# Scores of the narrow batches of a Nyström attention spread over all sixteen 32x32 tiles of the matmul engine

## The chip, the cores and the metric

The kernel runs on one core of one Trainium2 chip. The metric is device microseconds of one execution, compared by the median over runs. TensorE (PE) multiplies, with its weight loads listed apart (PEld); VectorE (DVE), ScalarE (ACT) and GpSimd (POOL) do the elementwise work; SyncE (SP) issues loads and stores, and GpSimd issues the loads of the expert weights.

## The reference, cut to what matters

Two stages follow one another. First comes Nyström attention over 8 batches, 8 heads, 576 tokens and head size 64, with 32 landmarks; a landmark is the mean of 18 consecutive tokens:

```
q_lm = q.reshape(B, H, m, S // m, D).mean(axis=3)      # m = 32, S // m = 18; k_lm likewise
A  = softmax(scale * q    @ k_lm^T)                    # 576 x 32
Bm = softmax(scale * q_lm @ k_lm^T)                    # 32 x 32
C  = softmax(scale * q_lm @ k^T)                       # 32 x 576
Z  = Bm^T / (norm1 * norminf); six times: Z = 2 Z - Z @ Bm @ Z
attn = A @ Z @ C @ v
```

Its output, one row of 512 for each of the 4608 tokens, goes into a mixture of 8 experts: a gate picks one expert for each token, and the token gets `gate * sigmoid * (relu(x @ w1[e]) @ w2[e])`. Inputs and outputs are float32.

## The kernel before, in words

**Batches and halves.** `attend(b, ...)` (line 631) handles one batch in two halves of four heads (`hf`). `solve` (line 830) iterates the inverse for a group of one or two batches; the groups are (0), (1), (2), (3), (4, 5), (6, 7). `finish` (line 936) routes a batch, has the weights of its most frequent expert brought, and computes that expert for the whole batch. Tokens that chose another expert are redone at the very end under a condition (lines 1193 on).

**Order of the work.** All operations are first registered with `P.op`, each with a cost for every engine that may do it, a priority and a load on the DMA queues. `Plan.run` (line 276) then lays out the whole program: it repeatedly takes the operation that can begin first on some engine, with ties broken by priority (`PR` for attention, `FR` for experts, and a table `OFF` with one offset for each operation), and picks the engine on which the operation would end first. The `shy` values add a penalty to one of the engines; `SHY = 1194.3494` ns is the penalty for putting a landmark sum on DVE instead of POOL. While PE would idle before 75 us, the planner puts in filler matmuls on a zero tile (line 572).

**Wide and narrow batches.** The first two batches (`PET = 2`) are wide: their q and k are transposed by PE, so that head size (64) lies on partitions together with the parity of the token, and scores contract over 64 rows at once. The other six are narrow, and the change is about them:

- *Loads* (`bring`, line 646, issued on SP). For q and k, partition = (head, landmark), and a partition holds the landmark's 18 tokens as one run of 18 x 64 floats (4608 bytes); one DMA for a half batch (line 652). For v, three DMAs with runs of six tokens (1536 bytes, line 649). Three buffers for each of q, k and v; at most four loads are in flight.
- *Transposes* (line 690, DVE). Blocks of 32x32 are turned, so that 32 of the head's 64 columns (half `j`) lie on a head's 32 partitions, with tokens along the free dimension.
- *Landmark sums* (`sums`, line 700): 18 tokens are added, on POOL by five additions (lines 704 to 708) or on DVE by one reduction (line 702). The result `s9` has 64 columns for each of q and k. Line 723 turns it into `lm`.
- *Scores* (`scores`, line 741): for each half of the tokens (`n`), half of the head size (`j`) and head (`h`) there are two matmuls of 32 rows, 32 columns and 288 moving columns, one for k into `pC` and one for q into `pA`:

```
def one(n, x, h, j, o, p, last):
    nc.tensor.matmul(p.t[o * m:(o + 1) * m, n, :U2], lhsT=l_of(...), rhs=t_of(...), start=(j == 0), stop=last)
...
one(n, "k", h, j, h, pC, j == 1)
one(n, "q", h, j, (h + 2) % HH, pA, j == 1)
```

Row block `h` of the array is used with column block `h` (k) and `(h + 2) % 4` (q): eight of the sixteen 32x32 tiles. A float32 matmul stands as two records in the trace, so a narrow score has 64 matmul records and 64 weight loads; a wide one has 32 of each, on eight tiles of 64x32.

After the scores, `C` goes through a maximum on DVE (line 760), an exponential on ACT (765), a transpose on PE (773) and the product with v (784, `pv`). `A` is turned by DVE (802), normalised by POOL and DVE (805 to 819), turned again (823) and kept as bf16 in `Ab` (602 or 604). The inverse is line 914 (`pinv`), the routing runs from 964 to 1037, the requests for weights are lines 579 and 582 (POOL), and the expert is in lines 1088 (`mix`), 1103 and 1114 (`up2`, `up`), 1131 and 1134 (`down`), 1143 or 1145 (scaling) and 1158 (output, SP).

Of the kernel before, what the change touches and what calls it, by code (L numbers as in the profile page):

```python
# [23 lines left out]
BF16 = mybir.dt.bfloat16  # L24
# [4 lines left out]
ADD = mybir.AluOpType.add  # L29
# [4 lines left out]
X = mybir.AxisListType.X  # L34
# [37 lines left out]
class Plan:  # L72
# [380 lines left out]
def kernel(  # L453
# [22 lines left out]
    HH = H // 2  # L476
    PT = 96
    NT = 5
    U2 = S // 2
    UP = NT * 128  # L480
    NH = S // 2
    SHY = 1194.3494
    SHYE = 106.9356
    SHYR = -121.5916
    SHYB = 336.6076
    PR = [-20.0647, -14.4829, -11.9595, -11.6984, -8.0902, -5.3768, 0.7543, 4.1562]
    FR = [8.161, 20.7685, 18.9146, 5.2084, 9.1678, 27.2014, 12.0329, 8.2172]
    PET = 2
# [785 lines left out]
```

## Time and profile before

| | |
|---|---|
| median of three runs | 249.31 us (245.78 to 250.73) |
| profiled execution | 249.05 us, span 247.4 us |
| granted PE clock, mean | 0.986 |
| DVE, ACT, POOL busy | 174.2, 150.2, 137.1 us |
| line 743 (scores), k and q: matmul records | 448 and 448 |
| DMA | 31057 packets, 48.96 MB, 198 GB/s on average |

The profile is one execution, recorded by the hardware. "Busy" counts the time in which an engine has an instruction in flight; for PE this is modelled from pipelined matmuls, so a busy PE can still be far from its peak. The chain is followed backwards from the last instruction: at each step to what released it, or to the instruction before it on its engine. In the rows of groups the columns are line, engine, operation, output <- input, shape, count, then busy microseconds, mean nanoseconds of one, and the idle time just before with what ended it. S and M are the two kinds of PSUM tiles.

### The profile page before, as it was taken

The page shows a single profiled execution, that of the slowest core. Times are in us where ns is not written, and L with a number is a line of the kernel's source. Part 1 is how long each engine was busy: PE and PEld are TensorE (multiplying, and loading weights), DVE is VectorE, ACT ScalarE, POOL GpSimd, SP SyncE. Part 2 cuts the span into 40 slices and gives each one's busy share as a digit, 9 for nine tenths or more (in the row PEclk, how much of TensorE's full clock was granted, in tenths as well). Part 3 has the DMA queues.
Part 4 walks back from the last instruction along what each step waited for, and adds up shares of the span by engine and source line. Part 5 has one row for each costly group of instructions (what it writes and reads, how often), then busy time and mean ns, then how long its engine had stood idle before and what let it go on. Part 6 is the DMA issues. An engine that isn't in the chain of part 4 may idle for free.

```text
span 247.4 us, 10058 instructions
## 1 busy us (share of the span) xinstructions
PE 227.4 (92%) x4155; PEld 140.5 (57%) x4156; DVE 174.2 (70%) x405; ACT 150.2 (61%) x371; POOL 137.1 (55%) x205
## 2 busy tenths in 40 slices
PE   8998989978997999999999998999999999999970
PEld 3667664645564455655576667766666565555530
DVE  3648879997998589997995789888672473334330
ACT  2667764458774568695696755854785495625330
POOL 2658966979598665867765598815450055020000
PEclk9999999999999799999999999999999999999996
DMA  6999999999999875984898466105990369999542
GB/s 247 273 324 267 297 245 223 216 292 301 269 221 248 230 226 151 235 279 123 227 317 212 133 151 174 29 3 87 192 238 27 86 101 207 231 252 236 150 128 70
DMA packets 31057, 48.96 MB, mean 198 GB/s; under 512 B 5408, under 2 KB 22816, under 8 KB 31008
## 3 DMA queue, kind: packets, MB, share of 16 engines
q1 hardware_dynamic: 19904, 37.34, 53.3%
q0 software_dynamic: 10720, 10.49, 26.7%
q8 instruction: 33, 0.54, 0.9%
q10 hardware_dynamic: 384, 0.46, 0.7%
q14 instruction: 16, 0.13, 0.2%
HBM read 61.90 MB, written 9.44 MB: 288 GB/s over the span
## 4 chain that ended last, share of the span: by engine, by line
PE 69%; DVE 12%; DMA 7%; ACT 5%; issue 3%; POOL 1%; POOLq 0%; DVEq 0%; ACTq 0%
PE M L1131 22%; PE S L743 9%; PE M L914 7%; PE M L1114 6%; PE S L1103 6%; DMA w<-in_moe_w_dram 5%; PE M L784 4%; DVE s L702 4%; PE S L773 3%; PE M L1134 3%; DMA nk<-in_k_dram 2%; PE M L964 2%; PE M L676 1%; PE S L1088 1%; DVE sm L816 1%
## 5 line engine op out<-in xcount | busy, mean ns | idle before, releaser
L1131 PE MATMUL M<-w,hT 128*128 128x512 bf16 x256 | 62.1, 383 | 0.2
L1131 PEld LDWEIGHTS <-hT 128*128 128x128 bf16 x256 | 23.7, 99 | 26.3 <-issue 3.3
L579 POOL DMA_DIRECT2D w<-in_moe_w_dram x26 | 13.0, 505 | 30.7 <-DVE M L1036 22.7
L1143 ACT ACTIVATE y<-M,co 128x512 f32<-128x512 f32 (+1 forms) x34 | 22.1, 655 | 12.9 <-PE M L1131 6.5
L743 PE MATMUL S<-Tk,lm 32*32 32x288 f32 (+1 forms) x448 | 29.3, 405 | 0.0
L743 PE MATMUL S<-Tq,lm 32*32 32x288 f32 (+1 forms) x448 | 28.8, 404 | 0.0
L914 PE MATMUL M<-X 32*32 32x96 f32 (+1 forms) x768 | 23.4, 243 | 2.6 <-ACT X L928 1.8
L810 POOL TENSOR_TENSOR At<-At,sm 128x576 f32<-128x576 f32 x16 | 18.6, 1164 | 10.6 <-DVE sm L789 8.2
L914 PEld LDWEIGHTS M<-X 32*32 32x32 f32 x768 | 16.2, 105 | 11.9 <-ACT X L928 6.6
L600 ACT ACTIVATE hT<-M 128x288 bf16<-128x288 f32 x44 | 17.4, 421 | 9.1 <-PE M L1114 8.8
L1114 PE MATMUL M<-Ab_all,U 128*128 128x288 bf16 x128 | 22.8, 287 | 0.0
L819 POOL TENSOR_TENSOR At<-At,sm 128x576 f32<-128x576 f32 x16 | 18.6, 1161 | 6.1 <-DVE sm L817 4.0
L1103 PE MATMUL S<-Ab_all,U 128*128 128x288 bf16 x128 | 20.9, 286 | 0.6 <-ACT U L602 0.5
L928 ACT ACTIVATE X<-M 128x192 f32<-128x192 f32 (+1 forms) x34 | 13.2, 387 | 13.2 <-PE M L914 12.7
L602 ACT CAST U<-S 128x1024 bf16<-128x1024 f32 x16 | 16.0, 1015 | 4.1 <-PE S L1088 4.1
L704 POOL TENSOR_TENSOR s<-nq 128x576 f32<-128x576 f32 x13 | 18.4, 1412 | 0.0
L743 PEld LDWEIGHTS S<-Tk,lm 32*32 32x32 f32 (+1 forms) x448 | 14.7, 105 | 6.4 <-issue 1.1
L705 POOL TENSOR_TENSOR s<-s 128x256 f32<-128x256 f32 x23 | 16.8, 729 | 1.8
L704 POOL TENSOR_TENSOR s<-nk 128x576 f32<-128x576 f32 x10 | 14.2, 1418 | 5.6 <-DMA nk<-in_k_dram 5.6
L760 DVE TENSOR_REDUCE sm<-S 128x1 f32<-128x576 f32 x16 | 11.9, 743 | 7.1 <-PE S L743 7.0
L572 PE MATMUL M<-idle 128*128 128x512 bf16 x59 | 15.8, 415 | 1.1 <-DVE idle L585 1.1
L606 DVE TENSOR_SCALAR hT<-M 128x288 bf16<-128x288 f32 x20 | 8.8, 449 | 11.4 <-PE M L1114 11.2
(133 smaller groups left out, 486.5 us busy)
## 6 DMA issues: line engine op xcount, KB each, us to landing
nk<-in_k_dram SPq DMA_DIRECT2D x16, 576.0 KB, 6.9
nq<-in_q_dram SPq DMA_DIRECT2D x16, 576.0 KB, 6.8
nv<-in_v_dram SPq DMA_DIRECT2D x48, 192.0 KB, 5.8
w<-in_moe_w_dram POOLq DMA_DIRECT2D x16, 512.0 KB, 16.9
out_dram<-y SPq DMA_DIRECT2D x122, 64.0 KB, 4.0
w<-in_moe_w_dram POOLq DMA_DIRECT2D x20, 256.0 KB, 9.9
w<-in_moe_w_dram POOLq DMA_DIRECT2D x3, 1024.0 KB
out_dram<-y SPq DMA_DIRECT2D x30, 32.0 KB, 4.4
```

The costliest lines, as they stand in the source:

```text
L600: nc.scalar.activation(out=dst(), in_=src(), func=RELU)
L602: nc.scalar.copy(dst(), src())
L704: nc.gpsimd.tensor_tensor(s3.t, n.t[:, :9], n.t[:, 9:], op=ADD)
L705: nc.gpsimd.tensor_tensor(s3.t[:, :4], s3.t[:, :4], s3.t[:, 4:8], op=ADD)
L743: nc.tensor.matmul(p.t[o * m:(o + 1) * m, n, :U2], lhsT=l_of(lm, wide, 0 if x == "k" else 1, h, n if wide else j), rhs=t_of(Ts[x], x, wide ...
L810: P.op({"POOL": 1115}, lambda e, At=At, st=st: nc.gpsimd.tensor_tensor(At.t, At.t, b_l(st.t[:, 8:8 + g]), op=SUB), r=[st["ax"]], w=[At[0]] ...
L819: P.op({"POOL": 1115}, lambda e, At=At, st=st: nc.gpsimd.tensor_tensor(At.t, At.t, b_l(st.t[:, 32:32 + g]), op=MUL), r=[st["as"]], w=[At[0 ...
L914: nc.tensor.matmul(pN.t[r_, u * W + lo:(u + 1) * W], lhsT=cur.t[r_, u, :m] if it else nx.t[r_, u], rhs=cur.t[r_, u, lo:], start=(it == 0 a ...
L1103: nc.tensor.matmul(ph.t[:, n, :NH], lhsT=Uw.t[:, hf, fc * 128:(fc + 1) * 128], rhs=Ab.t[:, hf, n * NH:(n + 1) * NH], start=(hf == 0), stop ...
L1114: nc.tensor.matmul(ph.t[:, :NH], lhsT=Uw.t[:, hf, fc * 128:(fc + 1) * 128], rhs=Ab.t[:, hf, n * NH:(n + 1) * NH], start=(hf == 0), stop=(h ...
L1131: nc.tensor.matmul(py.t, lhsT=hTs[fc].t[:, i * 128:(i + 1) * 128], rhs=w2.t[:, fc, :], **f)
L1143: nc.scalar.activation(out=y.t[:, :n], in_=py.t[:, :n], func=COPY, scale=com.t[:, i:i + 1])
```

## The change

Only narrow batches change their data layout. Partitions of q and k become (token half `a`, head parity `l`, landmark `r`), and a partition holds two heads with nine tokens each (runs of 2304 bytes), in two DMAs. Sixteen tiles are then addressed by the scores: row block 2n+l, column block 2hh+l for k, and its neighbour for q. A landmark's sum now lies in two halves on partitions 64 apart, so that new copies (ACT or POOL) bring each half to the other's partitions and an addition on POOL completes it; the landmark transpose covers 256 columns instead of 128. v is loaded with runs of three tokens in six DMAs. The head order of `pA`, and with it lines 953, 1086 and 1223, becomes `h ^ 1`. Output rows of the narrow batches follow the new token order. The planner's costs for the changed operations, its priorities, penalties and offsets are replaced as well. The two `Ag` tiles of the conditional end are taken from `hT`. The diff, without the offsets and the conditional end:

```diff
-    SHY = 1194.3494
-    SHYE = 106.9356
-    SHYR = -121.5916
-    SHYB = 336.6076
-    PR = [-20.0647, -14.4829, -11.9595, -11.6984, -8.0902, -5.3768, 0.7543, 4.1562]
-    FR = [8.161, 20.7685, 18.9146, 5.2084, 9.1678, 27.2014, 12.0329, 8.2172]
+    SHY = 167.6745
+    SHYE = 109.3114
+    SHYR = -145.2341
+    SHYB = 2451.9822
+    PR = [-26.8602, -20.7218, -20.3964, -10.8075, -9.8749, 3.0349, 6.2307, 13.5424]
+    FR = [4.6994, 24.0288, 15.8812, 17.8203, 24.5648, 28.2369, 14.8052, 5.6756]
...
-    FILL = 1.2174
+    FILL = 1.2515
-    AFF = 0.1761
+    AFF = 0.3677
...
+                        elif x == "v":
+                            i_ = [nc.sync.dma_start(out=n.t[w * m:(w + 1) * m, :, a * 3 * D:(a + 1) * 3 * D],
+                                                    in_=s_.rearrange("h (r a w t) d -> a w r h (t d)", a=2, w=3, t=3)[a, w])
+                                  for a in range(2) for w in range(3)]
+                        elif not wide:
+                            i_ = [nc.sync.dma_start(out=n.t[a * D:(a + 1) * D].rearrange("p (h t) d -> p h (t d)", h=2),
+                                                    in_=s_.rearrange("(h l) (r a t) d -> a (l r) h (t d)", l=2, a=2, t=g // 2)[a])
+                                  for a in range(2)]
...
+                        if not wide:
+                            f, o = n.t.rearrange("p (h t) d -> p h t d", h=2), s9.t[:, i].rearrange("p (h d) -> p h d", h=2)
+                            if e == "DVE":
+                                nc.vector.tensor_reduce(o, f.rearrange("p h t d -> p h d t"), axis=X, op=ADD)
+                                return
+                            a = s3.t[:, :8].rearrange("p (h t) d -> p h t d", h=2)
+                            nc.gpsimd.tensor_tensor(a, f[:, :, :4], f[:, :, 4:8], op=ADD)
+                            nc.gpsimd.tensor_tensor(a[:, :, :2], a[:, :, :2], a[:, :, 2:4], op=ADD)
+                            nc.gpsimd.tensor_tensor(a[:, :, 0], a[:, :, 0], a[:, :, 1], op=ADD)
+                            nc.gpsimd.tensor_tensor(o, a[:, :, 0], f[:, :, 8], op=ADD)
+                            return
...
+                    def cross(e, s9=s9, other=other):
+                        for a in range(2):
+                            o, i_ = other.t[a * D:(a + 1) * D], s9.t[(1 - a) * D:(2 - a) * D]
+                            if e == "ACT":
+                                nc.scalar.copy(o, i_)
+                            else:
+                                nc.gpsimd.tensor_copy(o, i_)
+                    P.op({"ACT": 570, "POOL": 800}, cross, r=[s9[0], s9[1]], w=[other[0]], prio=pr + .02)
+                    P.op({"POOL": 600}, lambda e, s9=s9, other=other: nc.gpsimd.tensor_tensor(s9.t, s9.t, other.t, op=ADD),
+                         r=[other[0]], w=[s9[0], s9[1]], prio=pr + .02)
+                    P.op({"DVE": 330}, lambda e, lm=lm, s9=s9: nc.vector.transpose(
+                        out=lm.t.rearrange("p x r -> p (x r)"), in_=s9.t.rearrange("p x d -> p (x d)")),
...
+                    for j in range(2):
                         for n in range(2):
+                            for l_ in range(2):
+                                r_ = slice((2 * n + l_) * m, (2 * n + l_ + 1) * m)
+                                for hh in range(2):
+                                    c = 2 * hh + j
+                                    for i, (x, p) in enumerate((("k", pC), ("q", pA))):
+                                        o = 2 * hh + l_ if x == "k" else (2 * hh + l_) ^ 1
+                                        f = Ts[x].t[r_, j, hh * U2:(hh + 1) * U2]
+                                        nc.tensor.matmul(p.t[o * m:(o + 1) * m, n, :U2], lhsT=lm.t[r_, i, c * m:(c + 1) * m],
+                                                         rhs=f.rearrange("p (w c r) -> p c w r", w=3, r=m) if x == "k" else f,
+                                                         start=(j == 0), stop=(j == 1))
-                P.op({"PE": 980 if wide else 1950}, scores, recs=64 if wide else 128,
+                P.op({"PE": 980 if wide else 1010}, scores, recs=64 if wide else 128,
```

More of the change, by code (lines that the diff above doesn't have):

```diff
@@ L636, in attend @@
             lms, ATs = lms_of[b], ATs_of[b] = [], []
+            wide = b < PET
             for hf in range(2):
@@ L657, in bring @@
                                               reason="loads in flight")
-                    loads[me] = P.op({"SP": 470 if x != "v" else 1350}, bring, w=[n[0]], prio=pr if x != "v" else pr + .15, lag=2000,
+                    loads[me] = P.op({"SP": (1350 if wide else 2650) if x == "v" else 470 if wide else 850}, bring, w=[n[0]], prio=pr if x != "v" else pr + .15, lag=2000,
                                       load=(2500.0 if x == "v" else LOAD), after=behind)
@@ L666, in attend @@
                 Ts = {"q": Val(t_T["q"]), "k": Val(t_T["k"])}
-                wide = b < PET
                 if wide:
@@ L689, in attend @@
                     for x in "kq":
-                        P.op({"DVE": 1265}, lambda e, T=Ts[x], n=ns[x], x=x: nc.vector.transpose(
-                            out=T.t.rearrange("p j (t r) -> p t j r", r=m) if x == "q" else
-                            T.t.rearrange("p j (t w r) -> p w t j r", t=6, w=3),
-                            in_=n.t.rearrange("p t (j c) -> p t j c", j=2) if x == "q" else
-                            n.t.rearrange("p (w t) (j c) -> p w t j c", j=2, w=3)),
+                        P.op({"DVE": 1265}, lambda e, T=Ts[x], n=ns[x]: nc.vector.transpose(
+                            out=T.t.rearrange("p j (t r) -> p t j r", r=m), in_=n.t.rearrange("p t (j c) -> p t j c", j=2)),
                             r=[ns[x][0]], w=[Ts[x][u] for u in range(3)], prio=pr + .01)
@@ L722, in attend @@
                 else:
-                    P.op({"DVE": 205}, lambda e, lm=lm, s9=s9: nc.vector.transpose(
-                        out=lm.t[:, 0], in_=s9.t.rearrange("p x d -> p (x d)")),
+                    other = Val(t_sw)
+                    def cross(e, s9=s9, other=other):
[10 more added lines that the diff above has]
+                        out=lm.t.rearrange("p x r -> p (x r)"), in_=s9.t.rearrange("p x d -> p (x d)")),
                         r=[s9[0], s9[1]], w=[lm[0]], prio=pr + .02)
@@ L730, in attend, with t_of @@
                 st = Val(t_sm)
-                def t_of(T, x, wide, n, h, j):
-                    if wide:
-                        f = T.t.rearrange("p a c -> p (a c)").rearrange("p (t c) -> p t c", c=128)[n * D:(n + 1) * D, :, h * m:(h + 1) * m]
-                        return f.rearrange("p (w c) r -> p c w r", w=3) if x == "k" else f
-                    f = T.t[h * m:(h + 1) * m, j]
-                    if x == "k":
-                        return f.rearrange("p (c n u) -> p n c u", n=2, u=PT)[:, n]
-                    return f.rearrange("p (t n r) -> p n t r", n=2, r=m)[:, n]
+                def t_of(T, x, n, h):
+                    f = T.t.rearrange("p a c -> p (a c)").rearrange("p (t c) -> p t c", c=128)[n * D:(n + 1) * D, :, h * m:(h + 1) * m]
+                    return f.rearrange("p (w c) r -> p c w r", w=3) if x == "k" else f
                 def scores(e, pC=pC, pA=pA, lm=lm, Ts=Ts, wide=wide):
-                    def one(n, x, h, j, o, p, last):
-                        nc.tensor.matmul(p.t[o * m:(o + 1) * m, n, :U2], lhsT=l_of(lm, wide, 0 if x == "k" else 1, h, n if wide else j),
-                                         rhs=t_of(Ts[x], x, wide, n, h, j), start=(j == 0), stop=last)
                     if wide:
@@ L748, in scores @@
                                 for n in range(2):
[L749 to L756 removed]
+                                    o = h if x == "k" else h ^ 1
+                                    nc.tensor.matmul(p.t[o * m:(o + 1) * m, n, :U2], lhsT=l_of(lm, True, "kq".index(x), h, n),
+                                                     rhs=t_of(Ts[x], x, n, h))
+                        return
+                    for j in range(2):
+                        for n in range(2):
+                            for l_ in range(2):
[9 more added lines that the diff above has]
+                P.op({"PE": 980 if wide else 1010}, scores, recs=64 if wide else 128,
                      r=[lm[0]] + [Ts[x][u] for x in "kq" for u in range(3)], w=[pC[0], pA[0]], hold=[EC, At, st],
@@ L779, in attend, with v_of @@
                 pV = Val(p_M, "attn", CAPA)
+                def v_of(c, wide=wide):
+                    return c if wide else c % 2 * 3 + c // 2
                 def pv(e, pV=pV, ECT=ECT, n=ns["v"]):
@@ L1186 @@
     U, Mb = t_U.tiles[0], pool.tile([128, 128], BF16, name="Mg")
-    Ab = [pool.tile([128, S], BF16, name=f"Ag{i}") for i in range(2)]
+    Ab = t_hT.tiles[FCH:FCH + 2]
     rows = pool.tile([128, B, NT], F32, name="rows")
```

37 lines of the change are left out of this document (17 added, 20 removed), and 263 rows, old and new, of the table OFF.

## The prediction

> **What bounds the kernel now.** I read the busy shares and the chain first, then busy time by stretches, then single groups. The page, PE being the matmul engine:
>
> ```profile
> PE 227.4 (92%) x4155; PEld 140.5 (57%) x4156; DVE 174.2 (70%) x405; ACT 150.2 (61%) x371; POOL 137.1 (55%) x205
> PE 69%; DVE 12%; DMA 7%; ACT 5%; issue 3%; POOL 1%; POOLq 0%; DVEq 0%; ACTq 0%
> ```
>
> The chain that ended last is PE for 69%. A busy PE includes filler matmuls (line 572), so the stages have to be told apart. Busy time in three stretches, then line 572 alone in the first two:
>
> ```profile
> 0.00:60.00 60.00, 52.81 (x976) 33.91 (x978) 44.53 (x89) 34.77 (x95) 43.34 (x70) 1.00 1.04 268
> 60.00:180.00 120.00, 115.47 (x2540) 72.77 (x2541) 102.43 (x238) 82.13 (x215) 82.17 (x120) 0.99 0.75 186
> 200.00:248.00 48.00, 39.43 (x293) 22.04 (x290) 16.94 (x46) 20.42 (x37) 7.98 (x12) 0.96 0.86 175
> ...
> 0.00:60.00 60.00, 15.83 (x59) 6.07 (x59) 1.00 1.04 268
> 60.00:200.00 140.00, 0.00 (x0) 0.00 (x0) 0.99 0.71 175
> ```
>
> Columns: length, busy PE, weight loads, DVE, ACT, POOL, then clock, DMA share, GB/s. Up to 60 us PE is not the limit: 15.83 us of its 52.81 is filler. From 60 to 180 us there is no filler and PE is busy 115.47 of 120; DVE has 102.43 (85%), ACT and POOL 68%. So between 60 us and the end a microsecond less of PE work can be a microsecond less of time, if the other engines follow. The pieces of the chain that matter:
>
> ```profile
> 29.81 1.21 PE S L743 x32
> 43.33 13.31 DMA w<-in_moe_w_dram
> 111.19 2.10 PE S L743 x64
> 118.78 2.10 PE S L743 x64
> 194.73 1.22 PE M L964 x32
> 231.53 6.91 PE M L1131 x32
> 238.44 1.01 PE M L1134 x16
> ```
>
> A narrow score (one half batch, batches 2 to 7) takes 2.10 us of the chain with 64 records; a wide one (batches 0 and 1), 1.21 us with 32. The last routing is at 194.73 us, and a pure expert stage follows it.
>
> **The scores: the gain.** Line 743 by stretches: the wide ones alone, then eleven of the twelve narrow ones:
>
> ```profile
> 0.00:40.00 40.00, 4.82 (x128) 1.99 (x128) 1.00 0.98 273
> 60.00:180.00 120.00, 24.54 (x704) 14.12 (x704) 0.99 0.75 186
> ```
>
> 4.82 / 4 = 1.21 us for a wide score, 24.54 / 11 = 2.23 us for a narrow one, neighbours' overlap included. Inside one narrow score:
>
> ```profile
> 48.40 0.42 PE L743 MATMUL S<-Tk,lm 32*32 32x288 f32 x4
> 48.51 0.44 PE L743 MATMUL S<-Tq,lm 32*32 32x288 f32 x4
> 48.64 0.42 PE L743 MATMUL S<-Tk,lm 32*32 32x288 f32 x4
> 48.75 0.44 PE L743 MATMUL S<-Tq,lm 32*32 32x288 f32 x4
> 48.88 0.42 PE L743 MATMUL S<-Tk,lm 32*32 32x288 f32 x4
> ```
>
> Eight records, one for each tile in use, repeat every 0.24 us: eight rounds for 64 records. The code before uses eight 32x32 tiles (rows h; columns h and h+2). After, row block is 2n+l and column block 2hh+l for k and its neighbour for q: sixteen different tiles, as many matmuls of the same size, hence four rounds. Four rounds less are 4 x 0.24 = 0.96 us a score, which leaves 1.14 us. The wide score is the nearest row: four rounds too, 1.21 us, with four tiles beside each other in each half of the rows, so four moving streams for a row block are already read at once there. Issue is no obstacle: a round now would need sixteen records in 0.24 us. Eleven scores lie after 60 us: 11 x 0.96 = 10.6 us. Ends: 11 x (2.10 - 1.21) = 9.8 and 11 x (2.23 - 1.21) = 11.2 us; I take 10.6. The twelfth lies at 48 us, where filler would take its place: nothing.
>
> The Trainium skill, page "TensorE: Matmul & The Clock Gate", section "Measured speedup vs the span model", gives 10.6 times for sixteen 32x32 tiles. An estimate from that page: 64 x 0.24 / 10.6 = 1.45 us for a score, and a gain of 11 x 0.65 = 7.2 instead of 10.6, a time of 244.0 instead of 240.6. The wide score's 32 records in 1.21 us with eight tiles lie at 6.3 times, nearly eight but for the start, so I follow the row.
>
> **The landmark sums and the crossing: added work off PE.**
>
> ```profile
> L705 POOL TENSOR_TENSOR s<-s 128x256 f32<-128x256 f32 x23 | 16.8, 729 | 1.8
> L704 POOL TENSOR_TENSOR s<-nk 128x576 f32<-128x576 f32 x10 | 14.2, 1418 | 5.6 <-DMA nk<-in_k_dram 5.6
> L706 POOL TENSOR_TENSOR s<-s 128x128 f32<-128x128 f32 x23 | 10.5, 456 | 1.8
> L708 POOL TENSOR_TENSOR s<-s 128x64 f32<-128x64 f32 x23 | 7.4, 321 | 1.8
> L702 DVE TENSOR_REDUCE s<-nk 128x64 f32<-128x1152 f32 x6 | 13.0, 2167 | 2.9 <-DMA nk<-in_k_dram 2.9
> L723 DVE STREAM_TRANSPOSE lm<-s 128x128 f32<-128x128 f32 x12 | 3.1, 275 | 0.0
> L802 DVE STREAM_TRANSPOSE At<-S 128x576 f32<-128x576 f32 x16 | 12.3, 767 | 0.6 <-PE S L743 0.6
> L602 ACT COPY lm<-M 128x256 f32<-128x256 f32 x3 | 1.1, 367 | 0.6 <-PE M L718 0.6
> ```
>
> A sum on POOL was 1418 + 729 + 456 + 2 x 321 = 3.25 us. Now it is 512 columns (between the rows of 256 and 576: 1.28 us) + 729 + 2 x 456 = 2.92 us, 0.33 less. On DVE it reads the same 1152 columns: 2.17 us, unchanged. Added for each score: two copies of 64x256 (bounded by ACT's 128x256: 2 x 0.37 = 0.73 us on ACT; on POOL at most 2 x 0.73) and one POOL addition of 128x256, 0.73 us. The landmark transpose grows from 128 to 256 columns: between 275 and 767 ns, 416, so 0.14 more on DVE. For twelve scores: DVE +1.7, ACT +8.8, POOL +8.8 less up to 24 x 0.33 = 7.9. From 60 to 180 us DVE then asks 104 of the 109.4 us that are left, 95%; ACT has 27 us of room in the shorter stretch and POOL as much, and the order may put evictions (lines 600 and 606) and sums on either side. I cost the work at nothing, covered by that room, but not the added latency. Sum to score grows by about 0.73 + 0.73 + 0.14 - 0.33 = 1.3 us. After 60 us another batch's expert matmuls fill PE while it passes; before 60 us nothing does. One narrow score feeds work there: 1.3 us at most, and I take 1.0. If all twelve showed it would be 15.6 us; less than nothing is excluded, since each path has one step more.
>
> **Transposes, tiles' order, planner.** Both big transposes now have q's form. They cost the same:
>
> ```profile
> L690 DVE STREAM_TRANSPOSE Tk<-nk 128x1152 f32<-128x1152 f32 x12 | 16.2, 1349 | 0.0
> L690 DVE STREAM_TRANSPOSE Tq<-nq 128x1152 f32<-128x1152 f32 x12 | 16.0, 1336 | 0.0
> ```
>
> The h^1 instead of h+2 in lines 953, 1086 and 1223 keeps count and size: nothing. All priorities, offsets and shyness values change; they move work without adding any.
>
> **Loads.**
>
> ```profile
> nk<-in_k_dram SPq DMA_DIRECT2D x16, 576.0 KB, 6.9
> nv<-in_v_dram SPq DMA_DIRECT2D x48, 192.0 KB, 5.8
> ...
> 46.85 1.28 SPq L649 DMA_DIRECT2D nv<-in_v_dram  x3
> 48.30 0.35 SPq L652 DMA_DIRECT2D nq<-in_q_dram  x1
> ...
> SPq L1158 <- ACT y L1143: 37.6, 13, 10.2
> ```
>
> The 24 narrow q and k loads become two DMAs each, and twelve v loads six instead of three: 24 x 0.35 + 12 x 1.28 = 23.8 us more on SP's queue. SP stood waiting 37.6 us for the outputs of line 1143, so its time is there; queued behind are outputs, whose buffers are six: nothing to 1 us, I take nothing. The runs halve, 4608 to 2304 bytes for q and k and 1536 to 768 for v. The v loads with 1536-byte runs land 576 KB no later than k with 4608-byte runs (5.8 us after issue, three issues 0.85 us apart, against 6.9), so q and k should lose nothing. 768 bytes has no row. At best nothing; at worst twice v's time per byte, in which case the first weight load (13.31 us on the chain, at DMA share above 1) could come 3 us later. I take nothing, by the nearest row.
>
> **Instruction fetch.** The chain has 3% "issue", and the page one queue of PE's size:
>
> ```profile
> q8 instruction: 33, 0.54, 0.9%
> ```
>
> 33 fetches for 8311 PE instructions, about 256 each. The twelve scores hold 1536 of them, now consumed twice as fast. If the waits (2.5% to 3%, some 6.5 us) grow with the speed of that 18%, it is 1.1 us more. Ends: nothing, and six fetches that each cost a whole saving, 5.8 us. I take 1.1, as most fetches fall elsewhere.
>
> **The sum.** The profiled execution took 249.05 us, span 247.4 and 1.65 around it; the median of the three runs is 249.31, 0.26 more. 249.05 - 10.6 + 1.0 + 1.1 = 240.55, say 240.6 us.
>
> **Rivals.**
>
> A. PE's freed time turns into waits. DVE at 95% of the shortened stretch cannot finish attention earlier, and expert work is not there to fill in. For it: DVE's 85% now. Against it: expert work for batches 4 and 5 still runs after 194.73 us, so there is stock to draw on. Four fifths lost: 249.05 - 2.1 = 247 us.
>
> B. Sixteen tiles do not run at once. Row blocks 2n and 2n+1 write the same PSUM bank in different partitions; if such writes excluded each other, each round would split in two and scores stay at 2.1 us. With the costs above: 249.05 + 1.0 = 250 us. Against it: the records at 48.40 us, where four row blocks already write one bank and eight records still repeat in 0.24 us; for it, that no row shows sixteen. The Trainium skill, page "TensorEngine Tiling (Array Packing)", section "Gotcha 1: PSUM Pressure", says that different row tiles cannot use one PSUM bank simultaneously; by that rule this rival would hold, and this trace disagrees with it for eight tiles.
>
> C. Slower: DVE becomes the bound. The value that keeps sums off DVE falls from 1194 to 168. If all 24 narrow sums went there, about fifteen more than the nine that it has now (six of k in the row above, and three of q), DVE takes on 15 x 2.17 + 1.7 = 34.3 us, some 31 of it after 60 us. Its room to 180 us is 120 - 102.4 = 17.6, so it decides from about seven moved sums. With all fifteen, attention ends 31 - 17.6 = 13.4 us later, near 209. After it stand two batches of experts, about 13 us until the weights land (the 13.31 above) and 8 us of end. A batch of experts is 37% of the chain over eight batches (lines 1131, 1114, 1103 and 1134 below): 0.37 x 247.4 / 8 = 11.4 us. So 209 + 22.9 + 13.3 + 8 + 1.65 = 255 us. Against it: the planner gives a sum to whichever engine ends first, and POOL, at 68%, would take sums back.
>
> ```profile
> PE M L1131 22%; PE S L743 9%; PE M L914 7%; PE M L1114 6%; PE S L1103 6%; DMA w<-in_moe_w_dram 5%; PE M L784 4%; DVE s L702 4%; PE S L773 3%; PE M L1134 3%; DMA nk<-in_k_dram 2%; PE M L964 2%; PE M L676 1%; PE S L1088 1%; DVE sm L816 1%
> ```
>
> **How the numbers follow.** Forecast 0.62, with its own range of 236 to 244: from 249.05 - 11.2 with no cost, less 2 us for a better order, to 249.05 - 9.8 + 5. Better still, under 236: 0.04. A 0.14, B 0.08, C 0.12. Faster by over 2% (below 244.3; 2% is about what a measurement tells from no change): 0.62 + 0.04 = 0.66; within 2%: A and B, 0.22; slower: C, 0.12. The range reaches from 235 to 251, over the forecast, A and B, and leaves out C.
>
> **What would show it.** Right: line 743's successor has 64 records in 1.1 to 1.3 us on the chain; after 60 us PE is still busy for 95% with no filler; the last routing comes a few us before 194.73 or at it, with less expert work behind it. Wrong: scores near 2 us (B); PE idle, or filler past 60 us, with DVE over 95% (A); more than seven extra sums in DVE's row for 128x1152 and a last routing past 200 us (C); first weights landing after 58 us (loads). The fetch term shows as "issue" between records of one score.

## The result, and the profile after

| | before | after |
|---|---|---|
| median of 4 runs, us | 248.25 (245.78 to 250.73) | 262.13 (261.04 to 263.46) |
| profiled execution, us | 249.05, span 247.4 | 261.04, span 259.4 |
| last routing on the chain, us | 194.73 | 206.35 |

The ratio is 1.0597, 95% interval 1.0483 to 1.0711: the changed kernel is slower, by 14 us, where a gain of 8 was forecast. Times are medians of all executions; a ratio leaves out executions that ran in a slower state, so it need not be the quotient of two medians, and where the two differ the text goes by the ratio.

The page of the changed kernel: busy time of each engine, then the chain that ended last by engine and by line:

```profile
PE 223.3 (86%) x4132; PEld 137.6 (53%) x4154; DVE 189.3 (73%) x412; ACT 155.2 (60%) x388; POOL 127.1 (49%) x181
...
PE 56%; DMA 26%; ACT 6%; issue 4%; DVE 2%; POOL 1%; SPq 1%; POOLq 0%; DVEq 0%; ACTq 0%
PE M L1174 20%; DMA nq<-in_q_dram 12%; DMA nk<-in_k_dram 8%; DMA nv<-in_v_dram 6%; PE M L1157 6%; PE M L957 5%; PE S L1146 5%; PE S L793 5%; PE M L1177 3%; PE M L827 3%; PE S L813 2%; ACT sw L756 1%; PE M L1007 1%; PE M L695 1%; PE S L1131 1%
```

PE did get 4.1 us less to do (223.3 instead of 227.4), and DMA went from 7% to 26% of the chain, with the loads of q, k and v as its three lines. Where the idle time lies shows in the stretch from 60 to 200 us, first of the kernel before:

```profile
60.00:200.00 140.00, 135.16 (x2891) 84.53 (x2889) 112.78 (x273) 94.97 (x241) 85.78 (x124) 0.99 0.71 175
```

and in the same view of the changed kernel (length, PE, weight loads, DVE, ACT, POOL, clock, DMA share, GB/s):

```profile
60.00:180.00 120.00, 104.01 (x2337) 65.89 (x2347) 103.67 (x228) 86.49 (x223) 81.94 (x112) 0.96 0.83 187
60.00:200.00 140.00, 123.60 (x2797) 78.56 (x2809) 118.07 (x255) 97.88 (x252) 86.79 (x118) 0.97 0.80 180
```

PE's idle time from 60 to 200 us grows from 4.8 to 16.4 us, by 11.6; the last routing comes 11.6 us later, and behind it 53 us follow as before. So the whole loss lies ahead of the last routing, and it is idle time of PE, not work. DVE is not full: 103.67 of 120. What PE waited for stands in the chain by time (start, length):

```profile
31.36 8.37 DMA nq<-in_q_dram
...
39.75 4.59 DMA nk<-in_k_dram
...
46.28 6.99 DMA nk<-in_k_dram
...
53.28 9.58 DMA nv<-in_v_dram
...
63.65 9.28 DMA nk<-in_k_dram
...
72.94 5.74 DMA nv<-in_v_dram
...
78.70 12.82 DMA nq<-in_q_dram
...
91.66 1.28 POOL s L723
...
136.30 3.31 issue
...
206.35 1.22 PE M L1007 x32
```

From 31 to 92 us the chain is one load after another. It ends at a landmark sum on POOL (line 723), for which POOL waits 10.4 us in three waits on loads of q, and after it come the steps that the change added. The timeline there (start, length, instruction, idle before it and its releaser):

```profile
91.66 1.27 POOL L723 TENSOR_TENSOR s<-nq 128x512 f32<-128x512 f32 x1 [4.05 <-DMA nq<-in_q_dram]
...
94.84 0.83 ACT L756 COPY sw<-s 64x256 f32<-64x256 f32 x2 [2.69 <-POOL s L726]
97.31 0.73 POOL L760 TENSOR_TENSOR s<-s,sw 128x256 f32<-128x256 f32 x1
...
101.57 0.42 DVE L762 STREAM_TRANSPOSE lm<-s 128x256 f32<-128x256 f32 x1
```

The copies, the addition and the transpose take 2 us together, yet 6.7 us lie between the start of the copies and the transpose. Over the eleven scores whose copies run on ACT it is 3.4 to 10.9 us, 7.5 in the mean. POOL and DVE hardly wait there (0.1 us of idle time ahead of all additions, 0.0 ahead of all transposes, in the rows below): other work lies between. The planner laid the steps apart so that the crossing would be covered, and that means that the sum, and the load ahead of it, is wanted that much earlier. The groups of the added work:

```profile
L756 ACT COPY sw<-s 64x256 f32<-64x256 f32 x22 | 8.9, 405 | 6.5 <-POOL s L726 5.5 <-DVE s L720 0.6
L760 POOL TENSOR_TENSOR s<-s,sw 128x256 f32<-128x256 f32 x12 | 8.8, 734 | 0.1
L762 DVE STREAM_TRANSPOSE lm<-s 128x256 f32<-128x256 f32 x12 | 5.0, 419 | 0.0
L723 POOL TENSOR_TENSOR s<-nk 128x512 f32<-128x512 f32 x9 | 11.5, 1276 | 0.7 <-DMA nk<-in_k_dram 0.4 <-DMA nq<-in_q_dram 0.2
```

These are near the sizes of the prediction: 0.41 us a copy (0.37 forecast), 0.73 the addition, 0.42 the transpose, 1.28 the first step of the sum. The scores themselves, line 793 from 60 to 200 us:

```profile
60.00:200.00 140.00, 20.14 (x704) 10.28 (x704) 0.97 0.80 180
```

11 scores at 1.83 us, where they took 2.23. That is 4.4 us of PE saved, not 10.6.

### The profile page after: what moved, and what is told of

Its sections match the earlier page's. It is cut to its first block, busy times and chain, and to the rows that moved or that the text cites. A ratio compares the mean times of both kernels' runs of the same rounds, so it can differ in the third digit from the quotient of the medians.

```text
span 259.4 us, 10165 instructions
## 1 busy us (share of the span) xinstructions
PE 223.3 (86%) x4132; PEld 137.6 (53%) x4154; DVE 189.3 (73%) x412; ACT 155.2 (60%) x388; POOL 127.1 (49%) x181
## 4 chain that ended last, share of the span: by engine, by line
PE 56%; DMA 26%; ACT 6%; issue 4%; DVE 2%; POOL 1%; SPq 1%; POOLq 0%; DVEq 0%; ACTq 0%
PE M L1174 20%; DMA nq<-in_q_dram 12%; DMA nk<-in_k_dram 8%; DMA nv<-in_v_dram 6%; PE M L1157 6%; PE M L957 5%; PE S L1146 5%; PE S L793 5%; PE M L1177 3%; PE M L827 3%; PE S L813 2%; ACT sw L756 1%; PE M L1007 1%; PE M L695 1%; PE S L1131 1%
## 5 line engine op out<-in xcount | busy, mean ns | idle before, releaser
L1174 PE MATMUL M<-w,hT 128*128 128x512 bf16 x235 | 60.4, 385 | 1.9 <-issue 1.0
L862 POOL TENSOR_TENSOR At<-At,sm 128x576 f32<-128x576 f32 x16 | 18.6, 1160 | 16.4 <-DVE sm L860 13.1
L957 PEld LDWEIGHTS M<-X 32*32 32x32 f32 x768 | 15.8, 104 | 16.4 <-ACT X L971 9.8
L971 ACT ACTIVATE X<-M 128x192 f32<-128x192 f32 (+1 forms) x35 | 13.6, 387 | 16.9 <-PE M L957 16.4
L793 PE MATMUL S<-Tk,lm 32*32 32x288 f32 x384 | 21.6, 431 | 0.0
L793 PE MATMUL S<-Tq,lm 32*32 32x288 f32 x384 | 21.1, 432 | 0.0
L610 ACT ACTIVATE hT<-M 128x288 bf16<-128x288 f32 x38 | 14.9, 418 | 5.4 <-PE M L1157 5.3
L616 DVE TENSOR_SCALAR hT<-M 128x288 bf16<-128x288 f32 x26 | 11.2, 452 | 9.1 <-PE M L1157 8.0
L813 PE MATMUL S<-I,EC 128*96 128x128 f32 x96 | 14.3, 286 | 2.8 <-ACT EC L805 2.6
L827 PE MATMUL M<-nv,ECT 96*32 96x64 f32 x768 | 15.0, 227 | 1.9 <-issue 1.5
L709 DVE STREAM_TRANSPOSE Tk<-nk 128x1152 f32<-128x1152 f32 x12 | 16.3, 1356 | 0.0
L709 DVE STREAM_TRANSPOSE Tq<-nq 128x1152 f32<-128x1152 f32 x12 | 16.0, 1342 | 0.0
L827 PEld LDWEIGHTS M<-nv,ECT 96*32 96x32 f32 x768 | 12.2, 113 | 6.9 <-ACT ECT L612 3.5
```

What stands on the lines that cost most here:

```text
L709: P.op({"DVE": 1265}, lambda e, T=Ts[x], n=ns[x]: nc.vector.transpose(out=T.t.rearrange("p j (t r) -> p t j r", r=m), in_=n.t.rearrange("p ...
L793: nc.tensor.matmul(p.t[o * m:(o + 1) * m, n, :U2], lhsT=lm.t[r_, i, c * m:(c + 1) * m], rhs=f.rearrange("p (w c r) -> p c w r", w=3, r=m) ...
L813: nc.tensor.transpose(pE.t[:PT, c // 3, (c % 3) * 128:(c % 3 + 1) * 128], in_=EC.t[:, c % 2, c // 2 * PT:(c // 2 + 1) * PT], identity=I128)
L827: nc.tensor.matmul(pV.t[h * m:(h + 1) * m, :D], lhsT=ECT.t[:, c, h * m:(h + 1) * m], rhs=n.t[:, h, v_of(c) * D:(v_of(c) + 1) * D], start=( ...
L862: P.op({"POOL": 1115}, lambda e, At=At, st=st: nc.gpsimd.tensor_tensor(At.t, At.t, b_l(st.t[:, 32:32 + g]), op=MUL), r=[st["as"]], w=[At[0 ...
L957: nc.tensor.matmul(pN.t[r_, u * W + lo:(u + 1) * W], lhsT=cur.t[r_, u, :m] if it else nx.t[r_, u], rhs=cur.t[r_, u, lo:], start=(it == 0 a ...
```

## The experiments

Two theories stood at the start. The first: the new loads are slower, and attention waits for them. The second: the added steps between sum and score (the crossing) hold attention up. Beside them stood the new order as a whole, and the size of the gain.

**What sixteen tiles are worth.** A kernel with only the score matmuls, on zeros, everything else left out. Each form ran five times, a row of independent matmuls ahead of each.

```
for j in range(2):                     # sixteen tiles
    for n in range(2):
        for l in range(2):
            for hh in range(2):
                for x in range(2): ... row block 2n+l, column block 2hh+l or its neighbour
```

> Only score matmuls on zero data (the rest of the computation is left out), each variant five times between filler matmuls. If the sixteen-tile score is limited by issue (a pair of weight load and matmul every 18 to 19 ns), the variants with sixteen tiles all take 1.2 us from first to last start, in any order of tiles, the strided k the same, and those with 144 and 32 columns take about as long. If it is limited by streaming or by shared PSUM banks, 144 columns take near half, and the variant in which each row block writes a bank of its own comes near 0.84 us (three rounds of 0.24 and the issue of the last). Eight tiles: 1.77 us as in the kernel before. The burst of six scores shows instruction fetch: over 1.6 us a score if fetch limits it.

Busy time of five scores of each form: eight tiles (line 87), sixteen (96), sixteen with a bank for each row block (122), sixteen with 144 columns (131) and with 32 (140):

```profile
0.00:265.00 265.00, 10.85 (x320) 5.44 (x320) 1.00 0.01 3
...
0.00:265.00 265.00, 8.01 (x320) 4.04 (x320) 1.00 0.01 3
...
0.00:265.00 265.00, 8.01 (x320) 4.04 (x320) 1.00 0.01 3
...
0.00:265.00 265.00, 5.61 (x320) 3.61 (x320) 1.00 0.01 3
...
0.00:265.00 265.00, 3.77 (x320) 3.15 (x320) 1.00 0.01 3
```

A score goes from 2.17 to 1.60 us: 0.57 saved, not 0.96. The order of the tiles and k's strided columns changed nothing, nor did a bank for each row block. From the first start to the last, 63 steps, it is 1.77 us with eight tiles and 1.20, 0.84 and 0.56 us with sixteen at 288, 144 and 32 columns. So a record costs 28 ns with eight tiles and 19, 13 and 9 ns with sixteen, and four rounds of 0.24 us is not what sixteen tiles reach. Six scores back to back took 1.58, 1.72, 2.11, 1.74, 2.76 and 1.89 us, each from its first start to its last end: between the matmuls there are holes, the longest of 1.17 us. Whether these are instruction fetches is not shown; no fetch record of this trace lies in the longest one.

**What PE time is worth.** In the kernel before, half of each narrow score's contraction is left out (32 records on eight tiles).

```diff
-for j in range(2):
+for j in range(1):
```

> The kernel before with the second half of each narrow score's contraction left out, so that 32 records instead of 64 run on the same eight tiles in the same order of work. A score then takes about 1.2 us instead of 2.17. If PE's time after 60 us is the time of the kernel, as the prediction said: 249 - 10.6 = 238 us. If freed PE time turns into waits for other engines: 245 to 248 us.

240.51 us, ratio 0.9689 (0.9592 to 0.9786). Line 743 in this kernel, 60 to 180 us:

```profile
60.00:180.00 120.00, 13.40 (x336) 5.78 (x321) 1.00 0.81 198
```

10.5 scores at 1.28 us, 0.95 less than the 2.23 before; for eleven scores 10.5 us of PE. By the ratio the time fell by 7.7: a microsecond of PE is worth 0.7. What took over shows in the chain of this kernel, where DVE, 12% before, has 24%:

```profile
PE 48%; DVE 24%; DMA 9%; ACT 8%; POOL 5%; issue 3%; SPq 0%; POOLq 0%; DVEq 0%; ACTq 0%
```

**The loads, one property at a time**, in the kernel before and in its order. First, the 24 narrow q and k loads in two DMAs of 64 partitions each, runs as long as before:

```diff
+i_ = [nc.sync.dma_start(out=n.t[a * D:(a + 1) * D],
+          in_=s_[2 * a:2 * a + 2].rearrange("h (r t) d -> (h r) t d", t=g)) for a in range(2)]
```

> The kernel before with each narrow q and k load cut into two DMAs of 64 partitions with the same runs of 4608 bytes; order of work unchanged. If loads into 64 partitions are the slow ones (about 240 instead of 390 GB/s, as the landings of the changed kernel suggest), a load takes 2.4 instead of 1.5 us and the time rises by 4 to 8 us. If the length of the runs does it, or the loads do not matter: within 1 us of before.

252.38 us, ratio 1.0165 (1.0057 to 1.0273). Second, two DMAs of all 128 partitions, with runs half as long:

```diff
+i_ = [nc.sync.dma_start(out=n.t[:, a * 9:(a + 1) * 9],
+          in_=s_.rearrange("h (r a t) d -> a (h r) t d", a=2, t=g // 2)[a]) for a in range(2)]
```

> The kernel before with each narrow q and k load cut into two DMAs of 128 partitions with runs of 2304 bytes; as many DMAs as in the changed kernel. If the number of partitions is what slows a load, this is within 1 us of before; if run length or the number of DMAs in flight does, it rises by 4 to 8 us.

248.36 us, ratio 1.0019 (0.9962 to 1.0075). Third, v in six DMAs with 768-byte runs, as the change has it:

```diff
-if x == "v":
+if x == "v" and b >= PET:
+    i_ = [nc.sync.dma_start(out=n.t[w * m:(w + 1) * m, :, a * 3 * D:(a + 1) * 3 * D],
+              in_=s_.rearrange("h (r w a t) d -> a w r h (t d)", a=2, w=3, t=3)[a, w])
+          for w in range(3) for a in range(2)]
```

> The kernel before with each narrow v load in six DMAs with runs of 768 bytes, as in the changed kernel; order of work unchanged. If only loads into half of the partitions with q and k are slow: within 1 us of before. If short runs, or many DMAs waiting for one another on SP, cost as well: 2 to 5 us more.

248.34 against 249.76 us, ratio 0.9890 (0.9818 to 0.9961): nothing lost. So neither the number of DMAs nor the length of their runs costs time here, and 64 partitions do. By the times alone the case is close, as the intervals of the first two edits overlap; the DMA traffic decides it. The DMA view from 20 to 60 us (all traffic, then the queue of these loads: packets, MB, share of 16 engines), of the kernel with 64 partitions, and the size and time of its k loads over the whole span:

```profile
DMA packets 5218, 9.49 MB, mean 237 GB/s; under 512 B 570, under 2 KB 4193, under 8 KB 5210
...
q1 hardware_dynamic: 3427, 7.64, 79.9%
...
nk<-in_k_dram SPq DMA_DIRECT2D x24, 288.0 KB, 6.6
```

of the kernel with 128 partitions and short runs:

```profile
DMA packets 6715, 10.58 MB, mean 264 GB/s; under 512 B 615, under 2 KB 4399, under 8 KB 6706
...
q1 hardware_dynamic: 4759, 8.55, 79.1%
...
nk<-in_k_dram SPq DMA_DIRECT2D x24, 288.0 KB, 5.9
```

and of the changed kernel:

```profile
DMA packets 6816, 9.37 MB, mean 234 GB/s; under 512 B 691, under 2 KB 4611, under 8 KB 6807
...
q1 hardware_dynamic: 5781, 8.26, 87.9%
```

With the queue busy for the same 79 to 80%, 64 partitions move 237 GB/s and 128 move 264. In the trace 288 KB land every 1.2 us with 64 partitions (31.89, 33.10, 34.33, 35.54, 36.77 us in the changed kernel), and every 0.75 us with 128 (31.18, 31.93, 32.62, 33.38, 34.12 in the second of these). The addresses in DRAM are not the cause: a DMA of the second edit and one of the change read the same bytes, one half of each landmark's tokens of four heads, and differ only in the partitions that they write and in the order of the runs. Nor is it a smaller number of engines: in both forms a load has sixteen separate landings. Each packet takes longer. From 30 to 70 us a packet of 2304 bytes takes 145 ns at the median in the changed kernel and 106 in the second edit, and one of 4608 bytes 299 ns in the first edit and 191 in the kernel before.

**The crossing in the old order.** Copies (times zero, so that the numbers stay) and the addition are issued with the landmark transpose, in the kernel before:

```diff
+for a in range(2):
+    nc.scalar.mul(other[a * D:(a + 1) * D], s9.t[(1 - a) * D:(2 - a) * D], 0.0)
+nc.gpsimd.tensor_tensor(s9.t, s9.t, other, op=ADD)
 nc.vector.transpose(out=lm.t..., in_=s9.t...)
```

> The kernel before with the crossing added to each narrow score's landmark step (two ACT copies of 64x256, here times zero, one POOL addition of 128x256, a transpose of 256 columns), emitted at the place of the landmark transpose; order otherwise unchanged, sums as before. If the crossing is covered by room on ACT and POOL, as the prediction said: 0 to 2 us more. If its latency and the in-order queues of ACT and POOL bring it onto the path: 5 to 10 us more.

273.01 us, ratio 1.1030 (1.0891 to 1.1169), some 25 us more. Its waits, of DVE and of POOL (us in total, times, longest):

```profile
DVE lm L731 <- POOL s L730: 27.2, 12, 5.1
```

```profile
POOL s L730 <- ACT sw L729: 16.5, 7, 5.9
```

The copies and the addition take 1.6 us a score. DVE waits 2.3 us a score at its transpose, POOL 2.4 us at each of seven additions behind ACT's queue, and all that stands behind them in those queues waits too. Issued right behind the second sum instead:

```diff
 def sums(e, ...):
     add(e, n, s9, s3, i)
+    done.append(i)
+    if len(done) < 2 or wide:
+        return
+    ... the two copies and the addition of the diff above
```

> As the kernel before with the crossing, but with copies and addition emitted right behind the second sum of a half batch rather than at the landmark transpose. If the 23 us of that run were waits of DVE at the transpose: 251 to 257 us. If POOL, held at the addition until ACT has come to the copies, is the cause: 262 us or more.

290.16 us, ratio 1.1656 (1.1561 to 1.1751): worse. In its trace POOL still waits 12.9 us at the additions, and now ACT too stands at the copies, ahead of its other work, until POOL has the sums:

```profile
ACT sw L711 <- POOL s L722: 27.8, 10, 4.2
```

**All of the change in the old order** (the planner sees the old operations and costs; loads, sums, scores and outputs are the changed ones, and the crossing is inside the transpose):

```diff
+def lm_all(e, lm=lm, s9=s9):
+    ... copies and addition of line 756 and 760
+    nc.vector.transpose(out=lm.t..., in_=s9.t...)
+P.op({"DVE": 205}, lm_all, r=[s9[0], s9[1]], w=[lm[0]], prio=pr + .02)
```

> All of the change's computation (loads, sums, crossing, sixteen tiles), but laid out with the planner's costs, priorities and offsets of before, the crossing emitted with the landmark transpose. If the new order of the work costs much of the 14 us: near before, 248 to 253 us. If the loads and the crossing cost it in any order: 255 to 262 us or more, as this order expects neither.

268.67 us, ratio 1.0812 (1.0600 to 1.1024). The new order is not what loses the 14 us: with it the same work takes 262.13, 6.5 us less, if anything (the intervals overlap).

**The changed kernel with one part undone.** The gates' negation moved behind an attention step on POOL:

```diff
-P.op({"POOL": 400}, lambda e: nc.gpsimd.tensor_scalar(...), w=[gates[0]], prio=pr + .5)
+flips.append(flip)
+P.op({"POOL": 400}, lambda e: None, w=[gates[0]], prio=pr + .5)
...
     nc.gpsimd.tensor_tensor(At.t, At.t, b_l(st.t[:, 32:32 + g]), op=MUL)
+    if flips:
+        flips.pop()()
```

> The changed kernel with the negation of the gate weights, for which POOL waits 10.5 us at the start, moved behind a later operation of batch 0 on POOL; all else in the same order. If POOL's standstill at the start delays batch 0 and with it everything: 4 to 8 us less than 262. If loads bound the first 90 us anyway: within 2 us of 262.

261.82 us, ratio 1.0575 (1.0430 to 1.0719): nothing. q and k loaded as before, in one DMA (the layout that the scores need is left out):

```diff
-elif not wide:
-    i_ = [nc.sync.dma_start(out=n.t[a * D:(a + 1) * D]..., in_=...[a]) for a in range(2)]
```

> The changed kernel with its narrow q and k loads replaced by those of before (one DMA, 128 partitions, runs of 4608 bytes); heads and token halves then lie mixed up in the narrow batches, so that their numbers are not the reference's, while every instruction behind the loads and the order stay. If the slow loads make the chain of DMA waits from 31 to 92 us and with it the loss: 248 to 254 us. If the loads explain no more than the 4 us that they cost in the order of before: 257 to 259 us. If they do not matter in this order: 261 to 263 us.

251.17 us, ratio 1.0093 (1.0029 to 1.0157). The ratio falls by 5.0 of the 6.0 points: the loads carry some 12 of the 14 us. Copies and addition left out, loads as changed:

```diff
-P.op({"ACT": 570, "POOL": 800}, cross, r=[s9[0], s9[1]], w=[other[0]], prio=pr + .02)
-P.op({"POOL": 600}, lambda e, ...: nc.gpsimd.tensor_tensor(s9.t, s9.t, other.t, op=ADD), ...)
+P.op({"ACT": 570, "POOL": 800}, lambda e: None, r=[s9[0], s9[1]], w=[other[0]], prio=pr + .02)
+P.op({"POOL": 600}, lambda e: None, r=[other[0]], w=[s9[0], s9[1]], prio=pr + .02)
```

> The changed kernel without the copies and the addition that complete the landmark sums (they are left out, landmarks of narrow batches then are half sums); order of the rest unchanged. If the crossing costs by itself, by its latency or by the ACT and POOL time it takes: 4 to 10 us less than 262. If the new order has made room for it, and the price is that sums and loads must come earlier: 0 to 3 us less.

259.34 us, ratio 1.0466 (1.0360 to 1.0573): about 3 us less, with intervals that overlap. Both undone, by the two diffs above together:

> Both edits at once (the loads of before, no crossing). If these two carry the loss, what is left is the gain of the sixteen tiles: 240 to 246 us. If the new order itself is slow: still 250 us or more.

249.93 us, ratio 1.0053 (1.0000 to 1.0106). With both costs gone, nothing of the gain is left. To see why, the sixteen tiles alone in the order of before (old loads of q and k, no crossing; against the version with everything in that order):

```diff
-elif not wide:
-    i_ = [nc.sync.dma_start(out=n.t[a * D:(a + 1) * D]..., in_=...[a]) for a in range(2)]
...
-for a in range(2):
-    nc.scalar.copy(other[a * D:(a + 1) * D], s9.t[(1 - a) * D:(2 - a) * D])
-nc.gpsimd.tensor_tensor(s9.t, s9.t, other, op=ADD)
```

> Sixteen tiles in the order of before, with the q and k loads of before and without the crossing (both left out, so that the numbers of narrow batches are not the reference's). A score takes 1.60 instead of 2.17 us. By the ratio that the halved contraction showed (7 us of time for 10.6 of PE): 0.57 x 11 x 0.7 = 4.4 us less than before, 243 to 245 us. If instruction fetch takes back what faster scores save: 247 to 249 us.

245.36 us, ratio 0.9901 (0.9843 to 0.9959). Line 768, its narrow scores, from 60 to 180 us:

```profile
60.00:180.00 120.00, 18.16 (x704) 9.75 (x704) 1.00 0.79 200
```

11 scores at 1.65 us, 0.58 less than before, 6.4 us of PE in all; by the ratio the time fell by 2.5. The chain of this kernel has DVE at 28%:

```profile
PE 58%; DVE 28%; ACT 6%; issue 3%; DMA 2%; POOL 0%; DVEq 0%; ACTq 0%; POOLq 0%
```

This kernel and the changed kernel with both costs undone (ratio 1.0053) do the same work; they differ only in its order and in the engines that the planner picked. Their intervals do not overlap, so the new order by itself costs 1.5 points, 3.8 us. Of the whole loss of 6.0 points, in this order of undoing, 5.0 go to the loads, 0.4 to the crossing and 1.5 to the new order, less the 1.0 that the tiles gain. Last, the changed kernel without slow loads, crossing and half of the contraction:

```diff
-for j in range(2):
+for j in range(1):
```

> As the changed kernel with the loads of before and without the crossing, and with half of each narrow score's contraction left out as well (32 records on sixteen tiles, about 0.9 us instead of 1.6). If PE bounds this order of work too: 11 x 0.7 x 0.7 = 5 us less than the run with the full scores, 244 to 246 us. If in this order the time is set elsewhere: 248 to 251 us.

247.28 us, ratio 1.0009 (0.9955 to 1.0063). Its scores (line 781) from 60 to 200 us:

```profile
60.00:200.00 140.00, 10.99 (x352) 3.63 (x352) 0.96 0.73 181
```

Against 20.14 us for the changed kernel's scores that is 9 us of PE less. By the ratios (1.0009 against 1.0053 with the whole contraction) it is 1.1 us of time, and the intervals overlap: PE hardly bounds the new order. From 60 to 180 us DVE is busy for 111.60 of 120 in this kernel, and its chain is DVE for a third:

```profile
PE 43%; DVE 34%; DMA 6%; issue 6%; ACT 4%; POOL 4%; SPq 1%; POOLq 0%; DVEq 0%; ACTq 0%
```

**Why 64 partitions are slow.** If two such DMAs could run beside each other, the second halves should gain from another queue:

```diff
-nc.sync.dma_start(
+(nc.scalar if a else nc.sync).dma_start(
```

> The changed kernel with the second half (upper 64 partitions) of each narrow q and k load issued on ACT's queue instead of SP's; order unchanged, ACT spends some 0.6 us on each of 24 issues and waits there for free buffers. If loads are slow because one DMA at a time feeds only 64 partitions, two queues feed both halves at once: a pair lands as fast as one load of 576 KB did before (1.5 instead of 2.4 us), and the time falls below 258 us unless ACT's waits eat it. If 64 partitions are slow for another reason, such as more and shorter pieces: landings as before, 262 us or more.

265.82 us, ratio 1.0743 (1.0596 to 1.0890): not faster, with landings 0.7 to 1.8 us apart in the profiled execution. ACT's queue has other work ahead of these issues, so this does not rule the idea out; it is not confirmed.

## Why the prediction was wrong, point by point

**The step that failed first: the loads.** "So q and k should lose nothing" compared run lengths, and on run lengths it was right (the second load experiment). But the rows compared were all DMAs to 128 or 96 partitions, and the change writes 64. The diff showed it, in `n.t[a * D:(a + 1) * D]`, and no row bore on it; it should have been an unknown with a bound. 0.45 us more for each of 48 DMAs is 22 us of queue time. In the old order 4 us of it show, in the new one about 12. The sign for it was named: first weights late. The first mix matmuls (line 1131) start at 61.1 us; before (line 1088) they started at 53.7. The first requests for weights went out 7 us later too, at 48.4 instead of 41.1 us, so the weights were late because the routing that POOL waits for came later.

**The crossing: right in size, wrong in its cover.** All durations were right to a tenth of a microsecond, and "the work at nothing" held only because the planner laid the steps far apart. In the old order it costs some 25 us. In the new order its own cost is about 3 us with the slow loads and 1 us without, neither of them clear of the noise. But the cover has a price: copies start 7.5 us ahead of the transpose, so sums and loads are wanted earlier. That this is why slow loads cost 12 us here and 4 there is inferred from the pairs of runs, not shown by itself; the run that would show it, the new order without the room for the crossing, was not made.

**The gain: 0.96 us a score was 0.57.** The prediction held a round's length fixed at 0.24 us, and for "Issue is no obstacle" it had no row: sixteen records in 0.24 us would be 15 ns each. They went out at 19 ns each, 1.20 us from first to last start for 64, then 0.40 for the last; a round of sixteen is 0.30 us. Why 19, the runs do not show; it is less with fewer columns. The nearest row, the wide score, keeps eight records at work and so said nothing on sixteen. The estimate from the Trainium skill, page "TensorE: Matmul & The Clock Gate", section "Measured speedup vs the span model", 1.45 us, lay nearer to the measured 1.60 than the row did. In the changed kernel the scores took 1.83 in the mean.

**"A microsecond less of PE work can be a microsecond less of time"**: it is 0.7 by leaving out work in the old order and about 0.1 in the new one. Best case 11 x 0.57 x 0.7 = 4.4 us; the tiles alone in the old order gave 2.5, so 0.4 for each microsecond of the 6.4. In all three kernels the chain goes over to DVE: 12% of it before, and 24, 34 and 28% there.

**The fetch term: 1.1 us was too small, if issue is fetch.** PE's waits on issue in the changed kernel:

```profile
PE M L891 <- issue: 5.6, 2, 3.3
...
PE M L827 <- issue: 1.5, 1, 1.5
...
PE M L957 <- issue: 1.1, 1, 1.1
PE M L1174 <- issue: 1.0, 5, 0.3
```

and in the kernel before:

```profile
PE M L1134 <- issue: 0.8, 1, 0.8
PE M L848 <- issue: 0.5, 1, 0.5
PE M L914 <- issue: 0.5, 1, 0.5
PE S L773 <- issue: 0.4, 1, 0.4
```

9.2 against 2.2 us in these groups, and one piece of 3.31 us on the chain. The chain's whole issue time is 4.4% against 2.5%, about 5 us more. The two largest pieces on the chain, from 132.24 and from 136.30 us, each overlap a fetch record (131.0 to 132.4 and 137.0 to 138.3 us). The number of fetches is 33, as before. The sign that was named, issue between the records of one score, hardly came: these start at most 0.4 us apart, and the long pieces lie at lines 891 and 827. That the scores' records are used up faster may be the reason; no run isolated it.

**The rivals.** A's sign came true in the changed kernel, PE idle between 60 and 180 us, with another cause and to a larger size: DVE was at 86%, not 95%. A's mechanism shows once loads and crossing are out of the way: DVE then has 28 and 34% of the chain and is busy for 107 and 112 of 120 us, in the two kernels above. B is false: sixteen tiles run together, in one bank. That answers the rule quoted there from the Trainium skill, page "TensorEngine Tiling (Array Packing)", section "Gotcha 1: PSUM Pressure": a bank for each row block gave the same 8.01 us. C named the side and one sign, a last routing past 200 us, but DVE took five more sums (14 instead of 9), under the seven from which C would decide, and was not full. Its count was off too: it took the nine for narrow sums, while those at 4.90 and 6.99 us are of a wide batch, and of the fourteen only eight are narrow.

**What stays open**: why a packet takes longer when a DMA writes only 64 partitions; what sets 19 ns a record; and what in the new order costs 3.8 us when slow loads and crossing are gone. No version here that computes the reference is faster than the kernel before by 2%; v in six DMAs comes nearest, with 0.9890.

## What to carry to other kernels

Count the partitions that a DMA writes before its runs: a load cut into two halves of the partitions can cost more than one cut into short runs. A step that "hides" behind other work has to be laid out earlier, and so its inputs are wanted earlier; ask at once which load stands ahead of it and how much slack that load has. Before extrapolating a rate from n tiles to 2n, look for a row in which 2n are at work, and put a factor below one on PE time even where PE is busy for 96%: with DVE at 85% beside it, a microsecond was worth 0.7 or less here. When the order of work is laid out anew for a change, run the old work in the new order as well: the order has a price of its own.

## What the runs showed of the hardware that was not expected

- 288 KB to 64 partitions land every 1.2 us (240 GB/s), to 128 partitions every 0.75 us (390 GB/s), on the same queue, with runs of 2304 bytes in both.
- 32x32 matmuls on sixteen tiles go out at 19 ns each with 288 columns, 13 with 144, 9 with 32; on eight tiles at 28 with 288.
- The granted clock fell in the changed kernel behind stretches in which PE's work was thin. Stretches of 4 us (length, busy PE, clock, DMA share, GB/s):

```profile
50.00:54.00 4.00, 2.40 (x66) 1.00 1.12 222
54.00:58.00 4.00, 2.44 (x96) 1.00 1.19 226
58.00:62.00 4.00, 2.90 (x41) 0.60 1.19 250
62.00:66.00 4.00, 4.00 (x144) 0.55 1.13 278
```

From 58 to 66 us PE runs at 0.60 and 0.55 in the mean, after eight microseconds in which it was busy for 60% and never idle for more than 1.1 us at a time. A narrow score there took 2.6 us. Thin work alone does not decide it: from 72 to 76 us PE was busy for only 1.95 of 4 us and the clock stayed at 1.00. Over the span the mean is 0.962 against 0.986 before, which is some 6 us of full clock more that were not granted (259.4 x 0.038 less 247.4 x 0.014), a part of them at the end where PE has nothing to do. How much of the 14 us this carries, no run isolates.
